# One pass fewer in the weight conversion, and the rounding of the weights' high part on VectorE

## The chip, the cores and the metric

The kernel runs on one core of a Trainium2 chip. The metric is the device time of one execution in microseconds (us). A core has five engines that run side by side, each with its own queue in fixed order: TensorE (PE in the profile; its weight loads are PEld), VectorE (DVE), ScalarE (ACT), GpSimd (POOL) and SyncE (SP, which here only issues DMA transfers). They wait for each other through semaphores.

## What is computed

Attention over 4 x 8 heads with 576 tokens each, where every row of scores keeps its 32 largest values; then two layers of a feed-forward block on the 2304 x 512 result.

```python
scores = scale * np.matmul(q, k.transpose(0, 1, 3, 2))
kth = np.partition(scores, -top_k, axis=-1)[..., -top_k:-top_k + 1]      # top_k = 32
scores = np.where(scores >= kth, scores, -1e9)
attn = softmax(scores)                                                   # written out there
x = np.matmul(attn, v)                        # heads side by side: 2304 x 512
h = np.maximum(x @ moe_w_in, 0.0);  x = h * h @ moe_w_out                # layer 0, 512 -> 2048 -> 512
h = x @ moe2_w_in;  out = np.maximum(0.01 * h, h) @ moe2_w_out           # layer 1
```

The four weight matrices are drawn in double precision and reach the chip as 64-bit words.

## The kernel before

**Top 32.** A tile is 128 rows of scores (128 x 576). For each of the 144 tiles DVE makes four MAX8 passes (line 867, eight largest values each) and three MATCH_REPLACE8 passes (line 869, takes those values out). ACT then subtracts and exponentiates (lines 321, 325), PE transposes the result (line 339, into PSUM banks named `att`), ACT copies it out (lines 344 and 346), POOL makes the low part of it (line 347), and PE multiplies it with the values (lines 425 or 436).

**Two-part numbers.** The later multiplications run in the reduced float32r format. An operand is split in a high part, rounded to float32r, and a low part, which is what the rounding left; three products (high x high, high x low, low x high) make up one.

**Feed-forward.** The 2304 rows are cut in six blocks. For each block and layer, sixteen steps go over 128 of the 2048 hidden columns each: `h` (line 619) is 12 matmuls, ACT applies the nonlinearity (lines 629 to 638, tiles `ga` and `gh`), POOL or DVE makes its low part (line 639, `gl`), and `acc` (lines 656, 658) is up to 12 matmuls. The weights of one step are a *chunk*, 128 x 1024: half of it goes into `wi`, half into `wo`.

**Weight conversion.** There are 32 chunks (16 steps of two layers), each converted once, when block 0 first needs it, two steps ahead of its use; the result goes to DRAM (lines 566, 567) and later blocks load it from there. A 64-bit chunk arrives as `wraw` (line 511, 1 MB, two buffers). Line 532: ACT turns the low words of the whole chunk into the last mantissa bits of a float32 (`wc`). Then, for each half chunk: line 541, ACT reads the high words as float32, scales them by 2^-112 and writes them into an `att` bank of PSUM (there are three such banks, shared with scores and transposes); line 547, DVE shifts that left by three and ORs it into `wc`; line 548, DVE ORs the sign bit in, a second pass over the same data; line 552, ACT rounds `wc` to float32r, the high part; line 553, POOL subtracts, the low part. The lists `STAGES` and `w_convert` set in which order the program hands these over, between the matmuls of a step.

**What sets the order.** The program is written by slots: a slot is one DVE pass of the top 32, and events (loads, scores, transposes) are attached to slots; between them the running feed-forward steps are handed out at a rate per slot. A scheduler then lays the instructions of every engine in a fixed order by priorities and by a timeline of its own. So an edit to the conversion can move instructions on all engines, and does.

Of the kernel before, what the change touches and what calls it, by code (L numbers as in the profile page):

```python
# [8 lines left out]
F = mybir.dt.float32  # L9
R = mybir.dt.float32r  # L10
U = mybir.dt.uint32
AF = mybir.ActivationFunctionType
OP = mybir.AluOpType
# [6 lines left out]
H_SCALE = 2.0 ** -112  # L20
# [66 lines left out]
def topk_attention_moe_moe2_kernel(  # L87
# [21 lines left out]
    PE, ACT, DVE, POOL, SP = nc.tensor, nc.scalar, nc.vector, nc.gpsimd, nc.sync  # L109
# [6 lines left out]
    def bank():  # L116
        return psum.tile([P, 512], F, tag="att", name="att", bufs=3)
# [4 lines left out]
    def behind(key):  # L122

        return tc.issue_after(cur[key].ins) if key in cur else ExitStack()
# [60 lines left out]
    for i in range(4):  # L185
        x = const if i < 2 else ahead
# [312 lines left out]
    def w_alloc(i):  # L499
        wi = pool.tile([P, 2, 512], R, tag="wi", name="wi", bufs=3)  # L500
        wo = pool.tile([P, 2, 512], R, tag="wo", name="wo", bufs=4)
        wt[i] = (wi, wo)
        return wi, wo
# [21 lines left out]
    def w_convert_steps(i):  # L525
        if i >= len(steps) or not fresh[i]:
            return
        w2 = w_alloc(i)
        raw = wraw.pop(i)
        if W64:  # L530
            b = pool.tile([P, 1024], U, tag="wc", name="wc", bufs=WCB)
            ACT.activation(b, raw[:, :, 0], AF.Copy, scale=L_SCALE, bias=L_BIAS)
            c = b.bitcast(F)
        else:
            c = raw
        v = [None, None]

        def high(x):
            if W64:
                v[x] = bank()  # L540
                ACT.activation(v[x], raw[:, x * 512:x * 512 + 512, 1].bitcast(F), AF.Copy, scale=H_SCALE)

        def bits(x):
            if W64:
                vu, bx = v[x].bitcast(U), b[:, x * 512:x * 512 + 512]
                with behind("dve"):
                    DVE.scalar_tensor_tensor(bx, vu, 3, bx, op0=OP.logical_shift_left, op1=OP.bitwise_or)
                DVE.scalar_tensor_tensor(bx, vu, 0x80000000, bx, op0=OP.bitwise_and, op1=OP.bitwise_or)  # L548

        def parts(x):  # L550
            w, cx = w2[x], c[:, x * 512:x * 512 + 512]
            ACT.activation(w[:, 0, :], cx, AF.Copy)
            POOL.tensor_tensor(w[:, 1, :], cx, w.bitcast(F)[:, 0, :], op=OP.subtract)

        yield 0
        for todo in STAGES:
            for fn, x in todo:
                dict(high=high, bits=bits, parts=parts)[fn](x)
            yield 0
# [292 lines left out]
    while slot <= last:  # L852
        p, i = divmod(slot, 16)
        if slot >= 0 and p < NPAIRS:
# [7 lines left out]
            x = i % 2  # L862
# [80 lines left out]
```

## Time and profile before

| | us |
|---|---|
| median of three runs (lowest, highest) | 1190.76 (1190.1, 1191.47) |
| the profiled execution | 1189.77 |
| its span, first to last instruction | 1188.0 |
| busy: PE, DVE, ACT, POOL | 1124.0, 872.1, 820.1, 744.8 |

The span falls in stages, which the shares over all of it hide: up to about 160 us attention alone; from 167 to 395 us the conversion of the weights beside block 0 and the attention that goes on; up to about 930 us attention and feed-forward side by side; from there feed-forward alone. "Busy" is the time in which an engine had at least one instruction under way. For PE, whose matmuls overlap, a busy engine is not one at its peak; the number of matmuls in a stretch says more. "Idle before, releaser" names what an engine waited for.

### The profile page before, as it was taken

Reading aid. Unit: us, or ns where it says so; the run is one execution under the profiler, and the core shown is the slowest. Engines: PE = TensorE matmul, PEld = TensorE weight load, DVE = VectorE, ACT = ScalarE, POOL = GpSimd, SP = SyncE. Lnnn points to the kernel's source line nnn. Section 1 sums busy time; section 2 is a strip of 40 time slices with the busy share of each in tenths; the row PEclk is TensorE's granted clock in tenths of the full one; section 3 lists DMA queues with packets and bytes.
Section 4 is the critical chain, followed back from the end, with each engine's and each line's share of the span. In section 5 each row is a group of like instructions: output and inputs, shape, how many; then the busy total and the mean of one; then the engine's idle time right before and its main releaser. Section 6 shows DMA issues by size and latency. Waiting matters only on the chain.

```text
span 1188.0 us, 20096 instructions
## 1 busy us (share of the span) xinstructions
PE 1124.0 (95%) x6376; PEld 985.5 (83%) x6376; DVE 872.1 (73%) x1828; ACT 820.1 (69%) x1823; POOL 744.8 (63%) x958
## 2 busy tenths in 40 slices
PE   5899977989899999999999999999999999999997
PEld 4777765868688899898998998788888899998996
DVE  7999999888886668999999999989997400110010
ACT  6999998899989667887676777556766743332322
POOL 7968846999879677677886775767665653002100
PEclk9999989999899999999999999999999999999999
DMA  9868756899999698799888888667776499779973
GB/s 307 287 216 276 264 187 230 312 334 333 394 353 360 199 336 293 240 346 371 312 264 296 286 283 287 217 219 219 232 234 215 151 326 334 256 252 351 346 258 119
DMA packets 108201, 329.53 MB, mean 277 GB/s; under 512 B 17216, under 2 KB 25408, under 8 KB 104000
## 3 DMA queue, kind: packets, MB, share of 16 engines
q1 hardware_dynamic: 105472, 323.53, 79.8%
q10 hardware_dynamic: 2624, 4.72, 1.1%
q8 instruction: 52, 0.85, 0.3%
q14 instruction: 53, 0.43, 0.1%
HBM read 257.03 MB, written 71.17 MB: 276 GB/s over the span
## 4 chain that ended last, share of the span: by engine, by line
PE 57%; DVE 21%; ACT 12%; DMA 5%; issue 2%; POOL 2%; ACTq 0%; SPq 0%; POOLq 0%; DVEq 0%
PE h L619 22%; PE acc L658 13%; DVE m L867 10%; PE acc L656 9%; DVE w L869 8%; PE att L425 3%; PE att L436 3%; PE att L339 3%; ACT e L321 2%; ACT stage L304 1%; PE sp L303 1%; ACT e L325 1%; DMA wraw<-in_w_dram 1%; DMA out_dram<-y 1%; ACT s L304 1%
## 5 line engine op out<-in xcount | busy, mean ns | idle before, releaser
L619 PE MATMUL h<-xh,wi 128*128 128x512 f32 (+2 forms) x1280 | 345.9, 344 | 9.7 <-ACT ga L629 4.5
L867 DVE MAX8 m<-w 128x8 f32<-128x576 f32 x432 | 315.1, 756 | 1.8
L619 PEld LDWEIGHTS h<-xh,wi 128*128 128x128 f32 x1280 | 225.4, 190 | 38.6 <-ACT ga L629 6.7
L639 POOL TENSOR_TENSOR gl<-ga,gh 128x512 fp32r<-128x512 f32 (+2 forms) x160 | 162.5, 1018 | 137.2 <-ACT gh L638 110.9
L869 DVE MATCH_REPLACE8 w<-m,w 128x576 f32<-128x576 f32 x288 | 215.2, 751 | 0.5
L619 PE MATMUL h<-xl,wi 128*128 128x512 f32 (+2 forms) x640 | 203.3, 338 | 0.0
L347 POOL TENSOR_TENSOR PTs<-whole,PTs 128x512 fp32r<-128x512 f32 x112 | 144.6, 1297 | 43.7 <-ACT whole L346 43.2
L656 PE MATMUL acc<-gh,wo 128*128 128x512 f32 (+2 forms) x768 | 156.5, 343 | 0.8 <-ACT y L674 0.5
L658 PE MATMUL acc<-wo,gh 128*128 128x512 f32 x576 | 152.1, 396 | 0.5 <-ACT gh L638 0.5
L656 PEld LDWEIGHTS acc<-gh,wo 128*128 128x128 f32 x768 | 127.4, 190 | 13.4 <-ACT y L674 0.7
L321 ACT ACTIVATE e<-s,m 128x576 f32<-128x576 f32 x144 | 112.9, 785 | 32.3 <-DVE m L867 27.4
L639 DVE TENSOR_TENSOR gl<-ga,gh 128x384 fp32r<-128x384 f32 x32 | 17.9, 559 | 152.1 <-ACT gh L638 149.4
L619 PEld LDWEIGHTS h<-xl,wi 128*128 128x128 f32 x640 | 120.0, 189 | 10.6
L636 ACT ACTIVATE ga<-h 128x512 f32<-128x512 f32 (+2 forms) x96 | 46.6, 491 | 116.3 <-PE h L619 114.8
L658 PEld LDWEIGHTS acc<-wo,gh 128*128 128x128 f32 x576 | 105.4, 188 | 21.2 <-ACT gh L638 0.9
L867 DVE MAX8 m<-s 128x8 f32<-128x576 f32 x144 | 104.3, 754 | 17.7 <-ACT s L304 15.2
L325 ACT ACTIVATE e<-e,nb 128x576 f32<-128x576 f32 x144 | 111.5, 782 | 1.8 <-POOL nb L315 1.7
L869 DVE MATCH_REPLACE8 w<-m,s 128x576 f32<-128x576 f32 x144 | 108.2, 752 | 0.6
L339 PE MATMUL att<-ident,e 128*128 128x128 f32 x576 | 90.1, 277 | 7.6 <-DVE wc L548 3.0
L334 POOL TENSOR_SCALAR e<-e,rc 128x576 f32<-128x576 f32 x112 | 82.5, 748 | 16.0 <-DVE rc L330 14.5
L656 PE MATMUL acc<-gl,wo 128*128 128x512 f32 (+2 forms) x384 | 88.3, 349 | 3.8 <-POOL gl L639 3.8
L631 POOL TENSOR_TENSOR ga<-ga 128x512 f32<-128x512 f32 (+2 forms) x80 | 66.3, 829 | 36.9 <-ACT gh L630 36.7
(90 smaller groups left out, 2117.4 us busy)
## 6 DMA issues: line engine op xcount, KB each, us to landing
wi<-wd SPq DMA_DIRECT2D x160, 512.0 KB, 5.1
wo<-wd SPq DMA_DIRECT2D x160, 512.0 KB, 5.0
wraw<-in_w_dram SPq DMA_DIRECT2D x32, 1024.0 KB, 7.9
sd<-stage SPq DMA_DIRECT2D x76, 288.0 KB, 3.3
s<-sd SPq DMA_DIRECT2D x76, 288.0 KB, 4.8
wd<-wi SPq DMA_DIRECT2D x32, 512.0 KB, 7.8
wd<-wo SPq DMA_DIRECT2D x32, 512.0 KB, 8.4
vd<-VT SPq DMA_DIRECT2D x16, 640.0 KB, 5.8
```

Source lines behind the costliest of these rows:

```text
L321: ACT.activation(t["e"], t["s"], AF.Prelu, bias=pr["m8"][:, i, 31:32], scale=-1.0, alpha=1.0 / FAR)
L325: ACT.activation(e, e, AF.Exp, bias=pr["nb"][:, i:i + 1], scale=-FAR, accum_out=pr["sum"][:, i:i + 1])
L334: POOL.tensor_scalar(e, e, pr["rc"][:, i:i + 1], 1.0, op0=OP.mult, op1=OP.mult)
L339: PE.transpose(ps[:, j * P:(j + 1) * P], t["e"][:, j * P:(j + 1) * P], ident)
L347: POOL.tensor_tensor(pts[:, 4:8, c:c + P], whole, pts.bitcast(F)[:, 0:4, c:c + P], op=OP.subtract)
L619: PE.matmul(two[r][:, 0:n], lhsT=ws[r][:, w, c * P:(c + 1) * P], rhs=x[c][y][:, 0:n], start=cnt == mine[0], stop=cnt == mine[-1])
L631: POOL.tensor_tensor(a[:, 0:n], a[:, 0:n], a[:, 0:n], op=OP.mult)
L639: (DVE if j >= GLD else POOL).tensor_tensor(gl[:, 0:n], a[:, 0:n], gh.bitcast(F)[:, 0:n], op=OP.subtract)
L656: PE.matmul(acc[c][:, 0:n], lhsT=wo[:, w, cs], rhs=g[:, 0:n], start=first, stop=last)
L658: PE.matmul(acc[c], lhsT=g[:, cs], rhs=wo[:, w, :], start=first, stop=last)
L867: cur["dve"] = DVE.max(out=m8[:, x, 8 * r:8 * r + 8], in_=t["s"] if r == 0 else t["w"])
L869: cur["dve"] = DVE.match_replace(out=t["w"], in_to_replace=m8[:, x, 8 * r:8 * r + 8], in_values=t["s"] if r == 0 else t["w"], imm_value=NEG)
```

## The change

The first scaling on ACT becomes a `Prelu` with slope 2^32 for negative inputs: it scales positive high words by 2^-112 as before and negative ones by 2^-80, so that after the shift by three the sign stands in the top bit by itself. The second DVE pass (line 548 of before) goes. The rounding to float32r leaves ACT and becomes a `tensor_scalar` (times one, times one) on DVE.

```diff
         def high(x):
             if W64:
                 v[x] = bank()
-                ACT.activation(v[x], raw[:, x * 512:x * 512 + 512, 1].bitcast(F), AF.Copy, scale=H_SCALE)
+                ACT.activation(v[x], raw[:, x * 512:x * 512 + 512, 1].bitcast(F), AF.Prelu, scale=H_SCALE,
+                               alpha=2.0 ** 32)
         def bits(x):
...
                 with behind("dve"):
                     DVE.scalar_tensor_tensor(bx, vu, 3, bx, op0=OP.logical_shift_left, op1=OP.bitwise_or)
-                DVE.scalar_tensor_tensor(bx, vu, 0x80000000, bx, op0=OP.bitwise_and, op1=OP.bitwise_or)
         def parts(x):
             w, cx = w2[x], c[:, x * 512:x * 512 + 512]
-            ACT.activation(w[:, 0, :], cx, AF.Copy)
+            DVE.tensor_scalar(w[:, 0, :], cx, 1.0, 1.0, op0=OP.mult, op1=OP.mult)
             POOL.tensor_tensor(w[:, 1, :], cx, w.bitcast(F)[:, 0, :], op=OP.subtract)
```

In the changed kernel one line more stands in `high`, so line 547 of before is line 548 there; line 552 is the rounding in both. DVE has as many instructions as before (64 passes fewer, 64 more), ACT has 64 fewer.

On ACT, before, in the middle of the conversion (two chunks; `wraw` is the raw chunk, `s_101` a tile of scores that DVE will search, `ga` and `gh` the hidden activations):

```order
L532 ACTIVATE wc<-wraw 128x1024
L552 ACTIVATE wi<-wc 128x512
L541 ACTIVATE att<-wraw 128x512
L629 ACTIVATE ga<-h 128x512
L552 ACTIVATE wo<-wc 128x512
L457 ACTIVATE xh_3222<-xf 128x256
L541 ACTIVATE att<-wraw 128x512
L304 ACTIVATE s_101<-att 128x288
L630 ACTIVATE gh<-ga 128x512
L552 ACTIVATE wi<-wc 128x512
L304 ACTIVATE s_101<-att 128x288
```

and in the changed kernel at the same tile of scores:

```order
L629 ACTIVATE ga<-h 128x512
L541 ACTIVATE att<-wraw 128x512 x2
L630 ACTIVATE gh<-ga 128x512
L532 ACTIVATE wc<-wraw 128x1024
L304 ACTIVATE s_101<-att 128x288 x2
L541 ACTIVATE att<-wraw 128x512
L344 ACTIVATE PTs<-att 128x4x128
```

The rounding passes that stood between the copies of scores and the activations are gone from ACT, and the two copies of a score tile stand side by side.

On DVE, before, a few chunks into the conversion (`m` and `w` belong to the top 32):

```order
L867 MAX m_2882<-w 128x8 x2
L548 SCALAR_TENSOR_TENSOR wc<-att,wc 128x512
L867 MAX m_3169<-s_104 128x8
L869 MATCH_REPLACE w<-m_2882,w 128x576
L869 MATCH_REPLACE w<-m_3169,s_103 128x576
L547 SCALAR_TENSOR_TENSOR wc<-att,wc 128x512
L867 MAX m_2882<-w 128x8
L547 SCALAR_TENSOR_TENSOR wc<-att,wc 128x512
L867 MAX m_3169<-w 128x8
L330 RECIPROCAL rc<-sum 128x2
L548 SCALAR_TENSOR_TENSOR wc<-att,wc 128x512
```

and in the changed kernel:

```order
L867 MAX m_2567<-w 128x8 x2
L548 SCALAR_TENSOR_TENSOR wc<-att,wc 128x512
L869 MATCH_REPLACE w<-m_2567,w 128x576
L869 MATCH_REPLACE w<-m_2870,s_101 128x576
L552 TENSOR_SCALAR wi<-wc 128x512
L867 MAX m_2567<-w 128x8
L867 MAX m_2870<-w 128x8
L869 MATCH_REPLACE w<-m_2870,s_102 128x576
L869 MATCH_REPLACE w<-m_2870,w 128x576
L548 SCALAR_TENSOR_TENSOR wc<-att,wc 128x512
L867 MAX m_2870<-w 128x8 x2
L552 TENSOR_SCALAR wo<-wc 128x512
```

Where a half chunk had two passes that read its `att` bank, it has one, and one pass from `wc` to `wi` or `wo` some places later.

On PE, before, behind the same four matmuls of `h` in block 1 (the 573rd to 576th of all; `e_107` to `e_110` are the four buffers of tiles to be transposed, used in turn):

```order
L619 MATMUL h<-xh_3222,wi 128x256 x4
L656 MATMUL acc<-gh,wo 128x256 x8
L339 MATMUL att<-ident,e_109 128x128 x4
L339 MATMUL att<-ident,e_110 128x128 x4
L303 MATMUL att<-KT,q_77 128x288
```

and in the changed kernel:

```order
L619 MATMUL h<-xh_3202,wi 128x256 x4
L303 MATMUL att<-KT,q_77 128x288
L303 MATMUL att<-KT,q_78 128x288
L436 MATMUL att<-PTs,VT 128x320 x8
L339 MATMUL att<-ident,e_107 128x128 x4
L339 MATMUL att<-ident,e_108 128x128 x4
```

At this place of the feed-forward work the changed kernel's order is one pair of tiles further in the attention: 60 tiles have been transposed there, 58 before.

## Rows read from the trace of the kernel before

**Rows 1.** The page: span, and part 1, busy time of each engine

```profile
span 1188.0 us, 20096 instructions
...
PE 1124.0 (95%) x6376; PEld 985.5 (83%) x6376; DVE 872.1 (73%) x1828; ACT 820.1 (69%) x1823; POOL 744.8 (63%) x958
```

**Rows 2.** Busy time by stage, all engines; the first line names the columns

```profile
core 0: us, PE busy (x) PEld busy (x) DVE busy (x) ACT busy (x) POOL busy (x), PEclk, DMA share, GB/s
160.00:210.00 50.00, 39.56 (x159) 27.68 (x158) 49.93 (x103) 42.50 (x92) 25.69 (x33) 0.87 0.59 206
210.00:320.00 110.00, 100.43 (x463) 80.42 (x461) 93.63 (x175) 100.84 (x190) 102.15 (x105) 0.97 0.96 340
320.00:420.00 100.00, 99.99 (x500) 83.62 (x501) 74.27 (x141) 82.42 (x154) 75.23 (x73) 1.00 0.86 308
...
480.00:720.00 240.00, 233.81 (x1453) 217.25 (x1452) 237.79 (x516) 178.57 (x399) 181.00 (x240) 1.00 0.88 302
```

**Rows 3.** Chain that ended last, 210 to 320 us, shares by line

```profile
by line: DMA wraw<-in_w_dram 15.2%; ACT att L541 8.4%; DVE m L867 7.6%; issue 7.4%; ACT wc L532 7.4%; DVE w L869 6.9%; DVE wc L547 6.6%; DVE wc L548 5.7%; ACT wo L552 4.9%; PE h L619 4.5%; ACT wi L552 4.1%; ACT e L321 3.7%; ACT gh L630 2.7%
```

**Rows 4.** Waits of PE, 210 to 320 us: total, times, longest

```profile
PE h L619 <- ACT ga L629: 2.3, 3, 1.1
PE att L339 <- ACT s L304: 1.8, 1, 1.8
PE att L339 <- DVE wc L548: 1.6, 1, 1.6
PE att L436 <- DVE PTs L364: 1.3, 1, 1.3
PE att L303 <- ACT s L304: 1.0, 1, 1.0
```

**Rows 5.** Timeline at 302 us: start, length, instruction, [idle before, releaser]

```profile
301.97 1.11 ACT L532 ACTIVATE wc<-wraw 128x1024 uint32<-128x1024 uint32 x1
...
303.85 0.40 ACT L304 ACTIVATE s<-att 128x288 f32<-128x288 f32 x1
...
304.30 0.66 PE L339 MATMUL att<-ident,e 128*128 128x128 f32 x4 [1.77 <-ACT s L304]
...
305.71 0.67 DVE L548 SCALAR_TENSOR_TENSOR wc<-att,wc 128x512 uint32<-128x512 uint32 x1
```

**Rows 6.** Groups by shape, whole span: busy us, mean ns, idle before

```profile
L344 ACT ACTIVATE PTs<-att 128x512 fp32r<-128x512 f32 x112 | 66.7, 595 | 30.9 <-PE att L339 30.3
...
L548 DVE SCALAR_TENSOR_TENSOR wc<-att,wc 128x512 uint32<-128x512 uint32 x64 | 42.7, 684 | 0.4
...
L541 ACT ACTIVATE att<-wraw 128x512 f32<-128x512 f32 x64 | 40.0, 636 | 0.9 <-DMA wraw<-in_w_dram 0.7 <-DVE wc L548 0.2
...
L552 ACT ACTIVATE wi<-wc 128x512 fp32r<-128x512 f32 x32 | 20.2, 632 | 5.5 <-DVE wc L548 4.0 <-ACT whole L346 0.8 <-ACT s L304 0.4
L552 ACT ACTIVATE wo<-wc 128x512 fp32r<-128x512 f32 x32 | 20.1, 630 | 0.6 <-PE acc L658 0.5
...
L636 ACT ACTIVATE ga<-h 128x512 f32<-128x512 f32 x32 | 18.8, 594 | 21.5 <-PE h L619 20.4 <-POOL PTs L347 1.1
...
L330 DVE RECIPROCAL rc<-sum 128x2 f32<-128x2 f32 x72 | 11.7, 162 | 7.7 <-POOL sum L329 7.6
```

**Rows 7.** Line 552 alone by stage: busy time of ACT

```profile
210.00:320.00 110.00, 19.91 (x32) 0.97 0.96 340
```

**Rows 8.** Line 548 alone by stage: busy time of DVE

```profile
210.00:320.00 110.00, 21.51 (x32) 0.97 0.96 340
```

**Rows 9.** Timeline of POOL at 257 us

```profile
257.12 1.30 POOL L553 TENSOR_TENSOR wi<-wc,wi 128x512 fp32r<-128x512 f32 x1
258.36 1.31 POOL L347 TENSOR_TENSOR PTs<-whole,PTs 128x512 fp32r<-128x512 f32 x1
259.61 1.31 POOL L553 TENSOR_TENSOR wo<-wc,wo 128x512 fp32r<-128x512 f32 x1
```

**Rows 10.** Chain that ended last, 480 to 720 us, shares by line

```profile
by line: DVE m L867 38.6%; DVE w L869 27.8%; PE acc L658 6.8%; PE h L619 6.7%; issue 3.3%; DVE PTs L364 3.0%; DVE xf L442 2.5%; PE att L436 2.1%; DVE xl L671 1.4%; PE att L303 1.3%; PE att L339 1.3%; ACT e L321 1.1%; ACT PTs L344 1.1%; ACT 
```

## The prediction

> **What bounds the kernel now.** I read the busy shares first [rows 1]: PE is busy 95% of the 1188.0 us span, so whatever another engine sheds returns at most what PE loses by waiting. Where PE loses is read by stage [rows 2]. The conversion lies in the first three stages shown. From 320 to 420 us PE is busy 99.99 of 100 us and passes 500 matmuls: nothing taken off another engine can shorten that stretch. From 210 to 320 us it is busy 100.43 of 110 us and passes 463. At the pace of the next stage these 463 would take 463 / 5.00 = 92.6 us, so at most 17.4 us lie here, 9.6 of them as plain idle time. From 160 to 210 us DVE is busy 49.93 of 50 us, so there only a shorter DVE queue would help.
>
> In the stage from 210 to 320 us no engine stands out: POOL is busy 102.15, ACT 100.84, PE 100.43, DVE 93.63 of 110 us, and the DMA share is 0.96 [rows 2]. The chain of waits says which delays were the last there [rows 3]: the conversion on ACT (lines 541, 532 and both parts of 552: 8.4 + 7.4 + 4.9 + 4.1 = 24.8%), the two bit passes on DVE (12.3%), loads of raw weights (15.2%), and POOL in none of the larger shares. PE's own waits agree [rows 4]: 5.1 of the 8.0 us listed are waits for an ACT copy or activation, 1.6 us for line 548 to give back a PSUM bank. One of them can be followed in the timeline [rows 5]: ACT does 1.11 us of line 532 and more of the conversion before the copy of scores at 303.85, and PE, which needs the bank that this copy empties, starts at 304.30 after 1.77 us idle. In-order queues make the delay: ACT had a copy for PE, behind conversion work.
>
> **The change, part by part.**
>
> ACT, first pass: Copy becomes Prelu on the same data. Two rows of one shape, Prelu at line 636 and Copy at line 344, show 594 and 595 ns [rows 6]; line 541 stays at 636 ns, cost nothing. Prelu already runs on ACT in the attention's subtraction, between its exponentials.
>
> ACT, rounding: 64 passes of 632 and 630 ns go [rows 6], 40.3 us in all; 19.91 us of them in the stage from 210 to 320 us [rows 7], where ACT falls from 100.84 to 80.9 us. In the other two stages the passes lie beside a saturated DVE or a saturated PE and return nothing.
>
> DVE, bit pass: 64 of 684 ns go [rows 6], 21.51 us in the stage [rows 8]. DVE, rounding: 64 passes of 128x512 from SBUF to SBUF come. The trace has no such instruction on DVE. Its price lies between the shortest DVE instruction shown, 162 ns for two columns (line 330), and 684 ns for as many columns in a two-input pass [rows 6]; a gain below zero is excluded, since an instruction cannot free its engine. I take 684 ns, the row of equal width. Then DVE's work is unchanged: minus 64 x 0.684 plus 64 x 0.684 = 0; at the other end it would shed 64 x 0.522 = 33.4 us, 16.7 us of it in the stage. What hides this difference is that DVE has 110 - 93.63 = 16.4 us to spare there [rows 2].
> The Trainium skill ("VectorE: DVE Perf Modes", section "The perf-mode tier table") gives a float32 tensor_scalar from SBUF to SBUF two elements a cycle, 1227 ns for 2048; an estimate from that page and the fixed 162 ns is (1227 - 162) / 4 + 162 = 428 ns, which would take 64 x 0.256 = 16.4 us off DVE. The sum below would stay as it is, since PE's waits for DVE in the stage are counted by the bank alone; no run here has shown that rate yet.
>
> The bank: `att` has three buffers, and each half chunk held one through lines 541, 547 and 548. Now line 547's successor frees it, at least one 0.67 us pass earlier (here 305.71 to 306.4 us [rows 5]). PE's 1.6 us wait for line 548 [rows 4] goes; I count 1.6 us.
>
> The copies and activations behind line 552: PE's waits for ACT are 5.1 us in five pieces, 1.0 us each on the mean [rows 4]. The rounding was 20% of ACT's work (19.91 of 100.84), and one or two passes of 0.63 us stood ahead of a late copy in its queue, as the ACT order of before shows. Bounds: 0 if ACT is late by line 532 and 541 alone, 5.1 if all go. A queue with 27% slack in place of 8% should seldom be late: I take 4.0 us.
>
> Rounding moved past DVE's queue: it waits only for the bit pass ahead of it on its own engine, and for a free `wi` or `wo` buffer. Before, ACT waited 0.5 us in all for such a buffer [rows 6], so what now queues behind that wait, the MAX8 passes, loses nothing that can be seen. No DMA is issued by the steps that move; SP issues the next raw chunk when line 541 has read the buffer, which comes earlier with a shorter ACT queue. What that triggers, loads and stores that start earlier, meets a DMA share of 0.96: I count nothing for it.
>
> Sum: 1.6 + 4.0 = 5.6 us. POOL, the next to be late, has 110 - 102.15 = 7.85 us of room in this stage, so the gain fits in below it. Behind the stage PE is the bound up to 420 us and carries the gain along. The profiled execution took 1189.77 us (1.77 us outside its span), 0.99 us less than the median of 1190.76. 1189.77 - 5.6 = 1184.2, on the scale of the median **1185.2 us**. With 2.4 to 10 us (part of the slow clock, 0.97 in this stage against 1.00 in the next, could come back too) the likeliest case alone spans 1180.8 to 1188.4.
>
> **The rivals.**
>
> *POOL and DVE get in each other's way: slower.* The new pass is an instruction that DVE does not have before, and POOL is nearly always at work beside it: 93% of the stage, passes of 1.3 us back to back [rows 2, 9]. If neither can pass while the other runs, each of the 32 rounding passes of the stage takes time from POOL. POOL has 7.85 us of room: from 7.85 / 32 = 0.245 us a pass it becomes the longest engine, and the low parts of `gh` and of the weights come late for PE. At half of a 0.684 us pass that is 32 x 0.342 - 7.85 = 3.1 us over, 1193.9 us; at the whole pass 14.0 us over, 1204.8 us. The other way round, a DVE pass that waits half a POOL pass, 0.65 us, costs DVE 20.8 us against 16.4 us to spare. For it: the load of both engines. Against it: POOL is not in the chain [rows 3], has 24.8 us to catch up with before 420 us [rows 2], and no row shows the two slowing each other.
> The Trainium skill ("SBUF — State Buffer", section "Who interferes with whom") states just this: VectorE's two-port modes, which a tensor_scalar can enter, and GpSimd share a port pair under an exclusive lock, and the one that comes second waits for the whole instruction of the other. By that and the 428 ns above, an estimate from pages, POOL would lose 13.7 us in the stage, 5.9 more than its room, which gives 1196.7 us. No row of before has such a pair of instructions at the same time, so the trace neither bears it out nor speaks against it.
>
> *Nothing that counts.* The five loads are so even that with ACT out of the way the raw loads (15.2% of the chain [rows 3]) and POOL keep the pace: 0 to 2.4 us, 1188.4 to 1193.1, about 1190. For it: POOL busier than ACT and the DMA share [rows 2]. Against it: PE's waits name ACT and line 548, not POOL or DMA [rows 4].
>
> *More than forecast.* From 480 to 720 us DVE is busy 237.79 of 240 us and its top-32 passes are 66% of the chain [rows 2, 10]. PE's new order is a pair of tiles further in the attention at the same feed-forward place; if DVE really gets that far ahead before 480 us, in its spare time, this stage shortens as well. All 17.4 us of the first gap would give 1173.4 us; half of the way between that and the forecast, 1179. Against it: an order promises work, it does not do it; if DVE does not get ahead, the same order makes PE wait.
>
> **How the numbers follow.** 2.4 us (0.2%) is about what a measurement of this kernel can tell from no change. Forecast 0.38, more than forecast 0.10, nothing that counts 0.22, slower 0.30. So faster 0.48, same 0.22, slower 0.30. Both signs hold much of the chance, so the range has to reach into both sides: from 1176, inside the larger gain, to 1199, half way between the two ends of the slower case; about two in ten are left outside.
>
> **What would show it.** In the changed trace, ACT from 210 to 320 us falls to about 81 us if the stage keeps its length; PE's waits for line 304 copies, for `ga` and for a DVE bit pass in that stretch fall from 6.7 us to about 1; line 552 on DVE shows 0.4 to 0.7 us. The slower case would show in POOL's low-part pass (line 553, 1.30 us) or DVE's line 552 growing well past these, POOL near 110 of 110 us and PE waiting for `gl` or `wi` from POOL. "Nothing" would show as the same 463 matmuls in the same 110 us with the waits under other names. I would be wrong in kind if the time changed mainly after 420 us, where I count nothing.

## The result: 1% slower

The changed kernel takes 1203.08 us (median of four runs, 1202.09 to 1205.49), the kernel before 1190.43 in the same comparison: ratio 1.010, 95% interval 1.0079 to 1.0121. The forecast was 1185.2 us and the range ended at 1199. The profiled execution, by the page of the changed kernel:

```profile
span 1200.3 us, 20050 instructions
...
PE 1128.4 (94%) x6376; PEld 989.6 (82%) x6376; DVE 873.8 (73%) x1828; ACT 789.8 (66%) x1759; POOL 755.8 (63%) x958
```

Against [rows 1] the span grew by 12.3 us. ACT is busy 30.3 us less. POOL, which the change does not touch, has gained 11.0 us with the same 958 instructions. By stage, columns as in [rows 2]:

```profile
160.00:210.00 50.00, 41.36 (x185) 30.39 (x185) 49.43 (x103) 39.27 (x85) 27.41 (x32) 0.93 0.59 203
210.00:320.00 110.00, 92.37 (x419) 73.38 (x417) 94.48 (x178) 84.47 (x156) 105.59 (x103) 0.93 0.96 347
320.00:420.00 100.00, 99.37 (x465) 81.95 (x466) 72.69 (x135) 67.08 (x122) 78.49 (x73) 0.98 0.81 288
```

In the stage that the forecast was about, ACT fell from 100.84 to 84.47 us, and still PE passes 419 matmuls where it passed 463. POOL, the fullest engine before as well, is at 105.59 of 110 us, and the mean granted clock is 0.93 where it was 0.97. PE's waits in this stage (total, times, longest), against [rows 4]:

```profile
PE acc L656 <- POOL gl L639: 12.1, 4, 4.9
PE h L619 <- ACT ga L629: 1.6, 1, 1.6
PE att L354 <- ACT s L304: 1.0, 3, 0.5
PE att L339 <- ACT whole L346: 0.8, 1, 0.8
PE att L339 <- ACT s L304: 0.7, 1, 0.7
```

The wait for the bank (line 548 of before) is gone; the waits for ACT are 4.4 us, with the 0.3 us that the view lists below these, where they were 5.1. A wait that was not there before, for the low part `gl` of the hidden activations from POOL, is 12.1 us. The longest piece can be followed. ACT's timeline has the `gh`, POOL's what runs until its `gl`, and PE's the wait:

```profile
244.54 0.61 ACT L630 ACTIVATE gh<-ga 128x512 fp32r<-128x512 f32 x1
```

```profile
245.78 1.06 POOL L257 TENSOR_TENSOR VT<-vraw,VT 128x320 fp32r<-128x320 f32 x1
246.80 0.74 POOL L460 TENSOR_TENSOR xl<-xf,xh 128x256 fp32r<-128x256 f32 x1
247.50 0.45 POOL L315 TENSOR_TENSOR nb<-m 128x2 f32<-128x2 f32 x1
247.91 1.29 POOL L639 TENSOR_TENSOR gl<-ga,gh 128x512 fp32r<-128x512 f32 x1
249.17 1.28 POOL L553 TENSOR_TENSOR wi<-wc,wi 128x512 fp32r<-128x512 f32 x1
250.42 1.30 POOL L553 TENSOR_TENSOR wo<-wc,wo 128x512 fp32r<-128x512 f32 x1
251.71 1.64 POOL L334 TENSOR_SCALAR e<-e,rc 128x576 f32<-128x576 f32 x2
253.31 1.04 POOL L631 TENSOR_TENSOR ga<-ga 128x512 f32<-128x512 f32 x1
254.30 1.30 POOL L553 TENSOR_TENSOR wi<-wc,wi 128x512 fp32r<-128x512 f32 x1
255.56 1.28 POOL L347 TENSOR_TENSOR PTs<-whole,PTs 128x512 fp32r<-128x512 f32 x1
256.81 1.45 POOL L553 TENSOR_TENSOR wo<-wc,wo 128x512 fp32r<-128x512 f32 x1
258.22 1.03 POOL L631 TENSOR_TENSOR ga<-ga 128x512 f32<-128x512 f32 x1
259.22 1.27 POOL L347 TENSOR_TENSOR PTs<-whole,PTs 128x512 fp32r<-128x512 f32 x1
260.45 1.27 POOL L639 TENSOR_TENSOR gl<-ga,gh 128x512 fp32r<-128x512 f32 x1
```

```profile
261.77 0.79 PE L656 MATMUL acc<-gl,wo 128*128 128x512 f32 x1 [4.87 <-POOL gl L639]
```

POOL is never idle here. The `gh` ends at 245.15, its `gl` starts 15.3 us later, and ahead of it in POOL's queue stand, among others, four low parts of coming weights (line 553, 5.3 us). Start of the `gl` less end of its `gh`, read in the same way for the sixth, seventh and eighth `gl`: 3.2, 6.0 and 4.4 us before, 11.8, 12.9 and 15.3 us in the changed kernel.

The new pass itself, by shape over the whole run:

```profile
L552 DVE TENSOR_SCALAR wo<-wc 128x512 fp32r<-128x512 f32 x32 | 23.5, 736 | 7.9 <-PE acc L658 6.3 <-PE acc L656 1.5
...
L552 DVE TENSOR_SCALAR wi<-wc 128x512 fp32r<-128x512 f32 x32 | 21.6, 677 | 0.6 <-PE h L619 0.4
```

Its single pieces run from 0.40 to 1.53 us. Here one pair falls into a POOL pass of a kind that takes 1.3 us elsewhere:

```profile
229.56 2.13 POOL L639 TENSOR_TENSOR gl<-ga,gh 128x512 fp32r<-128x512 f32 x1
```

```profile
229.80 0.40 DVE L552 TENSOR_SCALAR wi<-wc 128x512 fp32r<-128x512 f32 x1
230.12 0.41 DVE L552 TENSOR_SCALAR wo<-wc 128x512 fp32r<-128x512 f32 x1
```

So three causes offered themselves. **Theory 1, contention**: DVE's rounding and POOL hold each other up. **Theory 2, order**: the scheduler, given other instructions, laid out everything else differently, on POOL with the low parts of coming weights further ahead of `gl`. **Theory 3**: the wait for a free `wi` or `wo` buffer, 0.5 us on ACT before, is now 8.2 us (6.3 + 1.5 + 0.4 in the rows above) and stands in DVE's queue.

### The profile page after: what moved, and what is told of

Same layout as the page of the kernel before. It is cut to its first block, busy times and chain, and to the rows that moved or that the text cites. A ratio compares the mean times of both kernels' runs of the same rounds, so it can differ in the third digit from the quotient of the medians.

```text
span 1200.3 us, 20050 instructions
## 1 busy us (share of the span) xinstructions
PE 1128.4 (94%) x6376; PEld 989.6 (82%) x6376; DVE 873.8 (73%) x1828; ACT 789.8 (66%) x1759; POOL 755.8 (63%) x958
## 4 chain that ended last, share of the span: by engine, by line
PE 66%; DVE 11%; ACT 10%; POOL 5%; DMA 5%; issue 3%; SPq 0%; POOLq 0%; ACTq 0%; DVEq 0%
PE h L619 27%; PE acc L658 16%; PE acc L656 10%; DVE m L867 5%; PE att L436 4%; DVE w L869 4%; PE att L339 3%; PE att L425 2%; ACT e L325 2%; DMA wraw<-in_w_dram 1%; ACT stage L304 1%; PE sp L303 1%; ACT e L321 1%; PE att L303 1%; ACT s L304 1%
## 5 line engine op out<-in xcount | busy, mean ns | idle before, releaser
L619 PEld LDWEIGHTS h<-xl,wi 128*128 128x128 f32 x640 | 120.3, 189 | 10.5
```

What stands on the lines that cost most here:

```text
L619: PE.matmul(two[r][:, 0:n], lhsT=ws[r][:, w, c * P:(c + 1) * P], rhs=x[c][y][:, 0:n], start=cnt == mine[0], stop=cnt == mine[-1])
```

## Experiments

Ratios are to the kernel before, run beside each on the same chip, with 95% intervals.

**Each half of the change alone, and another form of the rounding.** First half alone (the rounding stays on ACT):

```diff
-            DVE.tensor_scalar(w[:, 0, :], cx, 1.0, 1.0, op0=OP.mult, op1=OP.mult)
+            ACT.activation(w[:, 0, :], cx, AF.Copy)
```

> Only the first half of the change: the high word goes through ACT as Prelu and VectorE makes one bit pass per half chunk; the rounding stays on ACT. The scheduler puts the low parts further ahead on POOL, as in the changed kernel: 12 of them stand ahead of the third gl, 17 ahead of the sixth (before 8 and 14, changed kernel 9 and 17). Theory 1 (VectorE's rounding passes and POOL's passes hold each other up): there is no such VectorE pass here, so the stall of acc behind gl in 210 to 320 us is gone (under 4 us, 12.1 in the changed kernel) and the time is 1183 to 1190 us. Theory 2 (low parts of coming weights queued ahead of gl on POOL): the stall stays, 8 us or more in this stage, and the time is 1195 to 1203 us. Theory 3 (the wait for a free wi or wo buffer now stands in VectorE's queue): as theory 1, 1183 to 1190 us.

1202.8 us, 1.0105 (1.0086 to 1.0124). It has no rounding on DVE, so nothing to contend with and no buffer wait in DVE's queue, and it loses as much as the whole change: neither theory 1 nor theory 3 is needed for a loss of this size. The time is the one that theory 2 named, but its mechanism did not come. The low parts stand further ahead, and still PE hardly waits for `gl` in the middle stage; it waits for ACT instead:

```profile
PE h L619 <- ACT xh L670: 3.6, 1, 3.6
PE att L339 <- ACT s L304: 2.5, 2, 2.3
...
PE acc L656 <- POOL gl L639: 0.2, 1, 0.2
```

So as a cause common to both kernels only the wide form of theory 2 is left: the new order as a whole costs the time, whichever wait it shows up in.

Second half alone (the sign pass on DVE and the `Copy` at line 541 stay):

```diff
+                DVE.scalar_tensor_tensor(bx, vu, 0x80000000, bx, op0=OP.bitwise_and, op1=OP.bitwise_or)
```

> Only the second half of the change: the high part is rounded by VectorE, and the two bit passes stay. The scheduler leaves the low parts on POOL where they were or later: 8 ahead of the third gl and 12 ahead of the sixth (before 8 and 14, changed kernel 9 and 17). Theory 1 (VectorE's rounding and POOL hold each other up): the rounding passes take 0.6 us and more in the mean (0.40 us when alone), POOL's busy time over the run grows by some 8 to 12 us as it did in the changed kernel (744.8 to 755.8), acc waits for gl in 210 to 320 us, and with VectorE's extra work the time is 1200 to 1212 us. Theory 2 (order on POOL): no stall behind gl, 1188 to 1195 us. Theory 3 (buffer wait in VectorE's queue): VectorE's rounding waits 5 us and more for acc to free wo, 1196 to 1206 us.

1212.0 us, 1.0175 (1.0155 to 1.0196), at the upper end of what theory 1 named; theory 2 and theory 3 missed (the rounding waits no more than 0.3 us for a buffer here). DVE is at 108.72 of 110 us in the middle stage, waits for POOL inside its passes included: a third pass per half chunk is too much for it. `acc` waits 5.3 us for `gl`, although the low parts stand no further ahead than before, so their place in POOL's queue cannot be all of it.

The changed kernel with a rounding that gives a second output:

```diff
-            DVE.tensor_scalar(w[:, 0, :], cx, 1.0, 1.0, op0=OP.mult, op1=OP.mult)
+            DVE.tensor_scalar(w[:, 0, :], cx, 1.0, None, op0=OP.mult, op1=OP.max,
+                              accum_out=pool.tile([P, 1], F, tag="rmax", name="rmax", bufs=2))
```

> The changed kernel with VectorE's rounding written as another form: one multiplication, with a running maximum for each partition as a second output that nobody reads. If this form runs at one column per cycle it takes some 0.6 us (the bit pass of 512 columns took about that), against 0.40 us of the form that it replaces when that one is alone. Its low parts on POOL stand as far ahead as in the changed kernel (10 ahead of the third gl, 16 ahead of the sixth). Theory 1 (the fast form and POOL hold each other up): the passes take nearly the same time each, with no long ones over 1 us, POOL's passes are back at the length of before (busy time 743 to 748 us), and the time falls to 1186 to 1194 us though VectorE has more to do. Theory 2 (order on POOL) and theory 3 (buffer wait in VectorE's queue): no better than the changed kernel, 1201 to 1210 us.

1192.1 us, 1.0003 (0.9989 to 1.0017). Its passes are even (shortest, median, longest in ns):

```profile
L552 DVE TENSOR_SCALAR_CACHE_REDUCE wi<-wc x32: 667/678/704, 171.9 to 396.9; 128x512 fp32r<-128x512 f32 x32
...
L552 DVE TENSOR_SCALAR_CACHE_REDUCE wo<-wc x32: 666/678/706, 172.5 to 398.2; 128x512 fp32r<-128x512 f32 x32
```

POOL's busy time is back at 745.3 us, and `acc` waits 0.9 us for `gl` in the middle stage, although the low parts stand nearly as far ahead as in the changed kernel. Taken alone this would look like proof of contention. But the scheduler had laid out this kernel differently again (of PE's 6296 scheduled instructions 2497 stand elsewhere than before, by 3.4 places in the mean; 4240 by 16.6 in the changed kernel). Order and form had to be separated.

**The disputed cost by itself.**

> No kernel of this case's computation: three forms of VectorE instructions and POOL's low part on 128 x 512 elements, 24 of each in a row, each on one engine alone or on both at once, and the output is not the reference's. Contention theory: the rounding form of the changed kernel takes 0.40 us alone, POOL's pass 1.30 us alone; with both at once one of the two, or both, grow, so that together they take about the sum (24 x 1.7 us = 41 us in place of 31 us, POOL's own). The form with a running maximum (0.68 us) and the bit pass that reads a psum bank (some 0.6 us) show no growth on either side: 24 POOL passes take 31 us beside them. Order theory: nothing is asked of it here; if there is no growth in the first pair, contention is out altogether.

Three views of this kernel. Line 104 is the rounding of the change, first alone (`a`), then beside POOL (`p`); line 114 is POOL's low part, the second row beside that rounding, the first row alone or beside the other two forms (number, then shortest, median, longest in ns). Then POOL's timeline, start and length of each block of 24 (alone, beside the rounding, beside the form with a maximum, beside the bit pass).

```profile
L104 DVE TENSOR_SCALAR d<-a x24: 417/427/427, 2.4 to 13.0; 128x512 fp32r<-128x512 f32 x24
L104 DVE TENSOR_SCALAR d<-p x24: 428/1366/1366, 45.7 to 76.9; 128x512 fp32r<-128x512 f32 x24
```

```profile
L114 POOL TENSOR_TENSOR p<-d,b x72: 1262/1262/1268, 13.5 to 177.5; 128x512 fp32r<-128x512 f32 x72
L114 POOL TENSOR_TENSOR p<-p,b x24: 1322/1322/1502, 45.7 to 78.1; 128x512 fp32r<-128x512 f32 x24
```

```profile
13.54 32.08 POOL L114 TENSOR_TENSOR p<-d,b 128x512 fp32r<-128x512 f32 x24 [13.10 <-DVE d L104]
45.70 33.70 POOL L114 TENSOR_TENSOR p<-p,b 128x512 fp32r<-128x512 f32 x24
96.98 32.13 POOL L114 TENSOR_TENSOR p<-d,b 128x512 fp32r<-128x512 f32 x24 [17.58 <-DVE d L107]
146.60 32.13 POOL L114 TENSOR_TENSOR p<-d,b 128x512 fp32r<-128x512 f32 x24 [17.48 <-DVE d L110]
```

Contention is real: the fast form grows from 0.427 to 1.366 us, one DVE pass per POOL pass, and POOL pays 1.6 us in 24 passes, 0.07 us each. The 41 us expected for both were wrong: they interleave within 33.7 us, nearly all of the loss on DVE's side. The other two forms, 0.69 us each (and 0.08 us more to read out the maximum), leave POOL at 32.1 us and are not slowed. The Trainium skill ("SBUF — State Buffer", section "Who interferes with whom") has this lock, and names `tensor_scalar` without an accumulator output as one that takes it; the trace agrees.

**Order and form apart.** An order is held by dependencies between neighbours in the list of one engine, without a semaphore; `_own` holds the instructions of each engine as the program issues them, `_seq` is the order wanted on engine `_e`:

```diff
...
+            for _x, _y in zip(_seq, _seq[1:]):
+                tc.add_manual_dep(_own[_e][_y], _own[_e][_x].name, _mybir.DependencyInfo(
+                    _mybir.DependencyClass.NoSync, _mybir.DependencyReason.DATA), reason="pinned order")
```

The changed kernel, PE, ACT, POOL and SP held to the order of before:

> The changed kernel with the order of the instructions on PE, ACT, POOL and SP held to that of the kernel before by dependencies that need no wait; VectorE's order is the scheduler's. Theory 1 (VectorE's rounding and POOL hold each other up): rounding passes still run up to 1.5 us, POOL's busy time stays 8 us and more above that of before, and the time is 1196 to 1206 us. Theory 2 (low parts ahead of gl on POOL): the stall of acc behind gl in 210 to 320 us goes (under 4 us) and the time falls to 1184 to 1191 us. Theory 3 (buffer wait in VectorE's queue): as theory 1, with VectorE's rounding waiting for acc as in the changed kernel.

1190.7 us, 0.9992 (0.9982 to 1.0003): all 12 us are back, as theory 2 had it, though the wait for `gl` falls to 5.3 us and not below the 4 it named. The contention is not gone: rounding passes take 0.82 and 0.87 us in the mean, more than in the changed kernel, and POOL is busy 753.6 us.

```profile
PE acc L656 <- POOL gl L639: 5.3, 5, 1.6
```

```profile
L552 DVE TENSOR_SCALAR wo<-wc 128x512 fp32r<-128x512 f32 x32 | 27.7, 867 | 3.9 <-PE acc L658 3.6
L552 DVE TENSOR_SCALAR wi<-wc 128x512 fp32r<-128x512 f32 x32 | 26.2, 822 | 0.4 <-PE h L619 0.2
```

The form with a maximum, in the same order:

> The changed kernel with VectorE's rounding in the form that took a steady 0.68 us beside POOL, and the order on PE, ACT, POOL and SP held to that of the kernel before. It differs from the changed kernel in the old order (1190.7 us) by the form of the rounding alone. Contention theory: POOL's busy time falls from 753.6 to 743 to 747 us, the remaining stalls of acc behind gl in 210 to 320 us (5.3 us in five pieces) go, and the time is 1186 to 1189 us. Order theory: the form counts for little once the order is held, 1189 to 1193 us.

1190.1 us, 0.9984 (0.9971 to 0.9998); the intervals overlap, and the wait for `gl` is 2.2 us. And the form with a maximum in the order of the changed kernel:

> The changed kernel's order on PE, ACT, POOL and SP, held by dependencies, with VectorE's rounding in the form that takes a steady 0.68 us beside POOL. It differs from the changed kernel (1203.1 us) by the form of the rounding alone, as the runs in the old order differ from each other (1190.7 and 1190.1 us). Contention theory (of the stall of acc behind gl, 12.1 us, a part is POOL's passes being stretched by the fast form): POOL's busy time falls from 755.8 to 743 to 747 us, the stall shrinks to under 5 us, and the time is 1193 to 1198 us. Order theory (the new order alone costs it): the stall stays and the time is 1200 to 1207 us.

1203.9 us, 1.0093 (1.0075 to 1.0112). POOL is at 744.5 us, no pass is stretched, and the loss stands. `acc` waits 8.8 us for `gl` (12.1 in the changed kernel): contention adds to that wait, but takes nothing more from the end that can be measured. Holding an order is not what makes a kernel fast or slow either: the form with a maximum takes, both times, about the time of the kernel whose order it was given. The middle stage of the first two, then PE's wait in the third:

```profile
210.00:320.00 110.00, 100.28 (x460) 79.93 (x460) 100.36 (x177) 85.03 (x158) 106.92 (x104) 0.97 0.95 342
```

```profile
210.00:320.00 110.00, 99.61 (x452) 79.02 (x450) 95.82 (x211) 84.29 (x157) 100.03 (x101) 0.95 0.96 344
```

```profile
PE acc L657 <- POOL gl L640: 8.8, 5, 3.8
```

The halves of the change in the old order, first half and second half:

> The first half of the change alone (Prelu, one bit pass), with the order on PE, ACT, POOL and SP held to that of the kernel before. Order theory: the 11 us that this half lost under its own order are gone; what the half is worth by itself is the waits for a psum bank in 210 to 320 us, 1.6 us at most, so 1187 to 1191 us. Contention theory has nothing to say against 1187 to 1191 us here either, but could not explain the 1202.8 us under its own order, since this half has no rounding on VectorE. If the Prelu itself were at fault (a slower read or a reload on ACT), the time would stay near 1200 us.

> The second half of the change alone (rounding on VectorE, both bit passes kept), with the order on PE, ACT, POOL and SP held to that of the kernel before. Order theory: most of the 20 us that this half lost is gone, 1190 to 1197 us. Contention theory: VectorE has both bit passes and the roundings, was 93.6 of 110 us busy in 210 to 320 us before and gets some 20 to 25 us of roundings there; it becomes the bound of that stage, with waits for wc and wi in PE's and POOL's queues, 1200 to 1212 us.

The first half takes 1190.9 us, 0.9991 (0.9977 to 1.0006): worth nothing that can be measured, and the `Prelu` is not at fault (line 541 at 635 ns). The second half takes 1208.7 us, 1.0137 (1.0115 to 1.0160), in the range of the contention theory and not in that of the order theory: here the order is not the cause, DVE's load is (104.57 of 110 us in the middle stage, 49.90 of 50 before it); how much of that load is waiting for POOL is not separated by a run. So the two halves do belong together: the pass that the first takes off DVE makes room for the rounding.

The reverse, the kernel before in the changed kernel's order:

> The kernel before, its instructions unchanged, with the order on PE, ACT, POOL and SP held to that of the changed kernel (the roundings on ACT, which have no place in that order, and VectorE's order are the scheduler's). Order theory (the changed kernel loses its time because the scheduler, given other instructions, puts the rest in another order): 1198 to 1206 us, with a stall of acc behind gl between 230 and 320 us and the later losses near 490 and 960 us as in the changed kernel. Contention theory (VectorE's rounding and POOL hold each other up, and the order matters little without that): 1188 to 1194 us. A third way, that holding any order changes the time by itself (by other waits): also off 1190.4, but then the equal-work lag would not have the places of the changed kernel.

1228.2 us, 1.0302 (1.0280 to 1.0324), far more than either theory expected, with other waits (from 210 to 330 us 5.3 and 3.5 us of PE for DVE's `wc`; 0.8 us for `gl`). That order has no place for the roundings on ACT, so this run says only that this order does not fit those instructions.

**Which queue.** POOL alone, then ACT alone, held to the order of before; the scheduler lays out the rest around it.

> The changed kernel with the order of POOL alone held to that of the kernel before (8 low parts ahead of the third gl, 13 of the fifth, 14 of the sixth, in place of 9, 14 and 17); the other engines' order is the scheduler's, which moves with it. If it is the low parts ahead of gl in POOL's queue that cost the time: the stall of acc behind gl in 210 to 320 us is under 5 us and the time 1189 to 1195 us. If the order of another engine costs it: 1198 to 1205 us.

> The changed kernel with the order of ACT alone held to that of the kernel before; POOL's order is the scheduler's (9 low parts ahead of the third gl, 16 of the seventh and so near the changed kernel's). If the conversions of coming chunks (wc and the high words) that ACT takes earlier are what costs the time: 1189 to 1195 us, and the late losses near 490 and 960 us go with it. If it is POOL's order: the stall of acc behind gl stays at 8 us or more and the time is 1198 to 1205 us.

POOL alone: 1202.4 us, 1.0077 (1.0052 to 1.0102). The low parts stand where they stood before, the stall behind `gl` is gone, and the time is not back. So the low parts ahead of `gl` are not what costs the end; PE waits elsewhere:

```profile
PE att L303 <- ACT s L304: 5.0, 3, 2.4
PE att L354 <- DVE wc L548: 2.3, 1, 2.3
...
PE acc L656 <- POOL gl L639: 0.8, 1, 0.8
```

ACT alone: 1190.2 us, 0.9997 (0.9981 to 1.0014), although on POOL 9, 11 and 16 low parts stand ahead of the third, fourth and sixth `gl`, nearly as in the changed kernel:

```profile
PE acc L656 <- POOL gl L639: 2.9, 2, 2.7
```

With ACT's order given, the scheduler's order on PE nearly returns to that of before as well (626 instructions elsewhere, by 0.5 places in the mean; 1627 by 2.1 with POOL held). So with ACT held nearly the whole layout comes back, and this run cannot say that ACT's queue alone is the cause; POOL's queue alone is not.

**Any new order, or this one?** Small pushes at the planner's numbers make the scheduler lay out the same instructions anew. The kernel before, the lead of the scores pushed either way:

```diff
-DLEAD = 30
+DLEAD = 28
```

> The kernel before, the same instructions, with the planner's lead of the scores 28 slots in place of 30. The scheduler then moves 2828 of PE's 6296 instructions, by 6.7 places in the mean (the change moved 4240, by 16.6). Draw theory (any new order is a fresh draw, and that of the kernel before is a good one): slower than before by 3 to 16 us, 1193 to 1207 us. Rival (it is the change that leads the scheduler to worse orders): 1188 to 1193 us.

> The kernel before, the same instructions, with that lead 32 slots in place of 30: 4013 of PE's instructions moved, by 10.8 places in the mean. Draw theory: 1193 to 1207 us. Rival (the change leads to worse orders): 1188 to 1193 us.

1192.8 us, 1.0020 (1.0004 to 1.0036), and 1195.4 us, 1.0029 (1.0018 to 1.0040). The changed kernel, with the same push and with another:

> The changed kernel, the same instructions, with that lead 28 slots in place of 30: 4535 of PE's instructions stand elsewhere than in the changed kernel, by 11.4 places in the mean. Draw theory: another time than 1203.1 us, anywhere in 1187 to 1210 us, and in the range of the pushed versions of the kernel before. Rival (the change leads to worse orders): 1199 to 1207 us, some 10 us above the pushed versions of the kernel before.

```diff
-SOON = 100
+SOON = 90
```

> The changed kernel, the same instructions, with one of the scheduler's priorities (SOON, line 66) at 90 in place of 100: 3151 of PE's instructions stand elsewhere than in the changed kernel, by 8.5 places in the mean; in the kernel before the same push moves none on PE. The low parts ahead of the first 24 gl on POOL and the conversions ahead of gh on ACT stand as in the changed kernel, so the order differs later than 320 us. Draw theory: the early stall of acc behind gl (12.1 us in 210 to 320 us) stays, the losses near 490 and 960 us (some 3 and 4 us) may go or grow: 1196 to 1208 us. Rival (the change leads to worse orders): 1200 to 1206 us.

1200.0 us, 1.0074 (1.0048 to 1.0100), and 1203.8 us, 1.0105 (1.0086 to 1.0124). Both theories were half right. The order of the kernel before is a good one, but pushing it costs 0.2 to 0.3%; the changed kernel lands 0.7 to 1.05% above in three layouts of its own, some 5 to 11 us above the pushed versions of the kernel before.

**Where in the run.** ACT's order of before held only up to the last rounding of the kernel before (near 400 us), and only behind it:

> The changed kernel with ACT's order held to that of the kernel before for the instructions up to the last rounding there (near 400 us), and left to the scheduler behind it. POOL's low parts and ACT's conversions ahead of each gl and gh stand as in the run with ACT's whole order held (1190.2 us). If the seat is the order among the conversions: the 8 us that the changed kernel has lost by 325 us at equal work are gone, and what stays is the draw of the later order: 1190 to 1196 us. If the later order is the seat: 1199 to 1206 us.

> The changed kernel with ACT's order held to that of the kernel before only for the instructions behind the last rounding there (from near 400 us on). The order among the conversions is the changed kernel's (15, 18, 21, 24 conversions on ACT ahead of the third to sixth gh, where the kernel before has 15, 15, 21, 22). If the seat is the order among the conversions: the stall of acc behind gl (12.1 us) and the 8 us lost by 325 us stay, the later 4 to 5 us go, and the time is 1196 to 1200 us. If the later order is the seat: 1189 to 1194 us.

1199.4 us, 1.0064 (1.0044 to 1.0084), and 1200.8 us, 1.0076 (1.0054 to 1.0098). Neither half of the order is the seat; each loses by itself. To see where, I compared the traces at equal work: every matmul counts with the distance to the next one that its shape usually has in the kernel before, and the table gives how much later than in that kernel the same sum is reached (us). These are single profiled executions: that of the first half alone is 3.2 us above its median, that with ACT's late order 3.1 us below, so a difference of 3 us between two columns says little.

| reached before at | changed | its order, form with maximum | old order | ACT old | ACT old, early only | ACT old, late only | first half alone |
|---|---|---|---|---|---|---|---|
| 251.7 | +0.4 | -1.7 | -2.4 | -0.9 | +1.7 | -0.4 | +2.2 |
| 325.3 | +8.0 | +7.8 | -0.4 | -0.3 | +2.6 | +7.8 | +7.1 |
| 428.2 | +7.8 | +8.7 | -0.2 | +0.2 | +5.4 | +8.4 | +6.5 |
| 513.7 | +12.0 | +14.1 | +0.2 | 0.0 | +6.5 | +8.4 | +10.7 |
| 920.8 | +8.6 | +10.4 | +0.7 | +1.3 | +6.6 | +8.7 | +12.0 |
| 1004.1 | +12.7 | +14.8 | +1.5 | +1.3 | +10.2 | +8.7 | +16.5 |
| 1166.9 | +11.8 | +14.7 | +0.6 | +0.4 | +10.5 | +7.8 | +15.9 |

The changed order loses some 8 us between 252 and 325 us, where the stall behind `gl` stands, and some 4 us in each of two later places, near 490 and near 980 us, where nothing of the change runs at all (PE's longest single waits there are 1.0 us for DVE's `xf` and 1.3 us for a load of weights); 3 us come back between, near 740 us. But a like early loss comes without that stall: the first half alone is 7.1 us late at 325.3, and by the same reckoning the run with POOL held is 6.5 and the changed kernel with lead 28 is 7.3 us late there, with waits for `gl` of 0.2, 0.8 and 1.0 us in the middle stage. With the late order of before the 8 us stay and the later losses go; PE's wait in the middle stage of that run:

```profile
PE acc L656 <- POOL gl L639: 13.9, 5, 5.1
```

With the early order of before the stall shrinks to 2.9 us and the 8 us become 2.6, but the later part is laid out anew and loses another 8.

## Why the prediction was wrong

**The step that failed is the sum's silent premise, that everything else keeps its order.** The sum, 1.6 + 4.0 us, prices what leaves ACT and DVE and puts the new places of all other instructions at nothing. They were listed under "The change" and weighed only where they could gain ("More than forecast"), with one clause that the order might make PE wait and no price for it. The price is 12 us: the same instructions take 1190.7 us in the order of before and 1203.1 us in their own. POOL's list did show, ahead of any run, the place where PE then waited: ahead of the third, fourth and sixth `gl` stand 8, 9 and 14 low parts before, and 9, 12 and 17 in the changed kernel, on an engine with 7.85 us to spare. But this count does not tell the time. The form with a maximum in its own layout (10, 12, 16) and the run with ACT's order held (9, 11, 16) are as fast as the kernel before; the first half alone (12, 13, 17) loses 11 us with hardly a wait for `gl`. The price is that of the whole layout, and the waits that carry it differ from one layout to the next.

**"POOL has 7.85 us of room, so the gain fits in below it."** With the order held, POOL takes 106.92 of 110 us, 4.8 us more than in [rows 2] with about as many passes (104 and 105). The room was not exceeded, but `acc` then waits 5.3 us for `gl` in five pieces. Room over a stage is an average: a queue that is 97% full over the stage was still late for `acc` five times.

**The bank, 1.6 us.** Gone in the changed kernel and in the old order, but with the first half in the old order 1.4 us of it are there, and with ACT's order held PE waits 3.4 us for line 548, now the only bit pass. Right in kind, not safe in size.

**The copies and activations behind line 552, 4.0 us.** Mis-sized. With the order held PE's waits for ACT in the middle stage are 3.2 us where they were 5.1; 1.9 us come back, and the wait for `gl` takes them. ACT itself shed its work nearly as computed, 84.47 us against the 81 forecast (85.03 with the order held). So with the order held the rival "Nothing that counts" describes the edit: 1190.7 us where it said about 1190.

**DVE's rounding, between 162 and 684 ns.** The upper bound did not hold: 677 and 736 ns in the mean, up to 1.53 us, because a wait for POOL counts as its length, as the 1.366 us beside POOL show. Taking 684 ns was nearly right for DVE's load by luck: it is some 0.40 us of work and some 0.3 of waiting. Alone the pass takes 0.427 us; the estimate in the prediction from the Trainium skill ("VectorE: DVE Perf Modes", section "The perf-mode tier table") was 428 ns, and the trace agrees.

**The rival "POOL and DVE get in each other's way"** named 1193.9 to 1204.8 us, and 1203.1 came. The number agrees by luck, since the mechanism does not carry it. POOL loses (753.6 - 744.4) / 64 = 0.14 us for each rounding pass in the old order and (755.8 - 744.5) / 64 = 0.18 us in the changed one, below the 0.245 us from which that rival was to decide, and taking the contention away moves the end by nothing measurable in either order (0.9992 and 0.9984; 1.0100 and 1.0093). The 13.7 us that POOL was to lose in the stage, by the estimate beside that rival, came out as 4.8 us with the order held.

**The buffer wait** was said to lose nothing. It is 8.2 us on DVE in the changed kernel, 3.8 us with the order held, where it does not cost the end. It was not tried alone; the first half alone loses as much without it.

**"Wrong in kind if the time changed mainly after 420 us"**: two thirds of it came before (7.8 of 11.8 us in the table), a third after, where the prediction counted nothing.

**What stays open**: why the scheduler lays out the changed kernel worse, and which feature of a layout decides. Of the seven layouts that the scheduler made for it, in whole or in part, six were 0.64 to 1.05% slower than the kernel before; the seventh, with ACT's order held, was not slower (0.9997). The form with a maximum, whose rounding is about as long as the bit pass it replaces, differs by 0.03%, which its interval does not tell from no change. Less work for DVE per half chunk may be what draws conversions forward, as the first half alone suggests (12 low parts ahead of the third `gl`); no run isolates that, and it would not by itself explain the time. No version measured here beats the kernel before by more than 0.2%.

## What to carry to other kernels

Where a scheduler sets the order, an edit is two changes: the instructions, and a new layout of all others. Run the edit once with the old order held, and the old kernel once with its layout pushed, before a gain or a loss is put down to the edit. What now stands ahead of an awaited result in the fullest queue points to a place where a wait can arise, but not to the time: here like counts came with and without the loss, and putting that one queue back moved the wait elsewhere. An order is judged by running it.

## What the hardware showed

- A DVE `tensor_scalar` of 128x512 float32 from SBUF to SBUF takes 0.427 us alone and 1.366 us (median) beside a stream of POOL passes that take 1.26 us alone; POOL grows by 0.07 us a pass. With a second, accumulated output the same pass takes 0.69 us, and neither side slows the other.
- Which side pays differs. In a dense stream DVE waited out each POOL pass. In the changed kernel a pair of 0.40 and 0.41 us ran unhindered inside a POOL pass whose record starts 0.24 us earlier, and that one took 2.13 us in place of 1.3.
- With the longer stalls PE's mean granted clock over the middle stage is 0.93 where it was 0.97; from 240 to 265 us, around the stall of 4.87 us, it is 0.82 where it was 1.00. From 260 to 266 us, where that stall ends, it is 0.50, the lower of the clock's two levels.
